# Re-laid seams between three phases of a spectral-mixer block, and its output bias added by VectorE

## The chip, the cores and the metric

The kernel runs on one core of a Trainium2 chip. The metric is the device time of one execution in microseconds (us), as the median of several runs. TensorE (PE) multiplies, VectorE (DVE) and ScalarE (ACT) work element by element, GpSimd (POOL) issues gathers and stores, and SyncE (SP) issues loads. Each engine takes its instructions strictly in order, and so does each DMA queue its issues.

## The reference, cut to what matters

The function is one transformer-like block, and the kernel computes its output and the gradients of all inputs. S is 2048 tokens, D 1024 channels, F 3584 hidden channels.

```python
h = _layernorm(x) * (1 + ca) + sa          # ca, sa, ga, cb, sb, gb: rows of silu(c) @ w_mod
x = x + ga * irfft2(rfft2(h) * W)          # W = w_r + 1j * w_i
h = _layernorm(x) * (1 + cb) + sb
y = _layernorm(h)
h = gelu(y @ w1 + b1)
x = x + gb * (h @ w2 + b2)                 # out_0; b2 is the output bias
```

Of the gradients, these matter here: that of row gb of the modulation is the sum over tokens of grad_out * (h @ w2 + b2); that of w2 is h^T @ (gb * grad_out); that of y is gz @ w1^T, where gz is the gradient ahead of the gelu.

## The kernel before, in words

The work goes through phases, all written as one program over four blocks b of 512 tokens (NB = 4, BW = 512); KH = 512 is half of the channels. The order of instructions on each engine is made by a scheduler from the order of the program, from priorities, and from explicit orderings: `ordered()` chains TensorE's products of the feed-forward phase (L650), `tc.high_priority()` lifts copies out of PSUM, `tc.issue_after` holds an instruction behind another. Tiles share memory by their tag, so a load into a new tile waits for the last reader of the old tile of that tag. PSUM has eight banks in three groups: `ps_s` (2), `ps_d` (2) and `ps_f` (4).

**Feed-forward, forward and local backward (L747 to L881).** `plan` (L853) is a list of steps. A "z" step (`z_block`, L762) computes one group of 512 hidden channels for a block: 32 products `pz` into four banks, copies by ScalarE (L779), then a long chain of ScalarE and VectorE for gelu and its derivative (L781 to L797), with stores of the hidden tile (`hh`, to d_hh) and of gz (to d_gz). A "b" step advances `bo_pass(b, h)` (L803), which multiplies hidden tiles by w2 for half h of the output channels. One pass has four banks `pbs`. It first adds the bias with four one-row products, one for each bank (L808: a row of ones times `b2_row`, a tile of one partition), then does seven groups of 16 products (L817), each with a w2 tile of 512 KB loaded into one of four slots `w2p` (L812). At the end ScalarE copies the banks to `bo` in the tile `otile` (L826), VectorE computes `go = grad_out * bo` (L827) and the output `bo * gb + x1` (L828, L829), which is stored. The second half of the generator, run later, sums `go` over tokens with four products `pa` against ones (L836), and VectorE adds the sum to `gacc` (L839, L841). These late parts are kept in `bo_late` and run at the first or second step of the next pass (L873); those of the last pass run at L879 and are followed by `store_gmod`, which sends gacc to memory as row 5 of d_gmod. `otile` is one tile, used by every pass.

**Gradient of y, the `pg` phase (L944 to L1029).** w1 is loaded transposed (L949). For each block and half, seven groups of 16 products `pg` (L996) accumulate in four `ps_f` banks from the gz tiles `gzr` (loaded at L989, eight slots) and w1T. ScalarE copies them out with sums (L1001), then VectorE runs two LayerNorm backwards (`ln_bwd`, L893, with L895 to L900 and L1017), and TensorE adds column sums of gn3, pru and au into the banks `acc3` (L193), placed by the scheduler among the next block's products. `got` is a scratch tile that also holds grad_out for the block (loads L128 on SP and two gathers L131 on POOL); `au` holds another operand. Beside this runs the "early" ring, `gmod_ring((5,), ...)` (L918): it loads row 5 of d_gmod to all partitions (L926), and goes through eight pieces of w_mod (L923), each with one VectorE product with a sum (L934), one scaled copy (L936) and a store by POOL (L937).

**Gradient of w2, the `gw2acc` phase (L1032 on).** Four tiles `gB` hold gb * grad_out, one for each block: loads on SP (L128), gathers on POOL (L131), then one VectorE product (L1037). They use the memory of w1T_0 to w1T_3, so each load waits until `pg` has last read that part. The generator `pieces()` (L1113) gives the work in pieces that `fill(n)` places between other phases: for each of 28 slices `fc` of the hidden channels, a transposing load of a 512 KB slice of d_hh (`hh_load`, L1115, on SP), and for each half h 16 products over the 16 token tiles t (L1090), tiles 4b to 4b+3 from gB block b, followed by a copy and a store. At the end of `pg` come six such pieces, then the last column sums (`sums3`), then ten pieces, then the backward spectral phase, which begins with the products `pu` (L451).

Of the kernel before, what the change touches and what calls it, by code (L numbers as in the profile page):

```python
# [11 lines left out]
BF16 = mybir.dt.bfloat16  # L12
I32 = mybir.dt.int32
ACT = mybir.ActivationFunctionType
ALU = mybir.AluOpType
AX = mybir.AxisListType

P = 128
S = 2048
D = 1024  # L20
# [10 lines left out]
NB = 4  # L31
# [4 lines left out]
def kernel(  # L36
# [135 lines left out]
    def tt(out, a, b, op):  # L172
        return nc.vector.tensor_tensor(out=out, in0=a, in1=b, op=op)  # L173
# [476 lines left out]
    def ordered():  # L650
        return tc.issue_after(last_pe[0].ins)
# [92 lines left out]
    n3Ts = [reg.tile([P, NDC, BW], BF16, name="n3Ta", tag="uv3")]  # L744
    otile = []

    b2_row = small.tile([1, D], BF16, name="b2_row", tag="gmrow", bufs=1)  # L747

    def after_ph():
        nc.sync.dma_start(out=b2_row[:], in_=B_b2.rearrange("(o n) -> o n", o=1))  # L750
        t2, t3 = (reg.tile([P, 2, 4, BW], BF16, name=f"gt{k}", tag=f"t{k}") for k in (2, 3))
        gts.append([t2[:, 0], t2[:, 1], t3[:, 0], t3[:, 1], uvp2[:, 0]])
        w2p.append(reg.tile([P, 4, BW], BF16, name="w2sB", tag="ph")[:])
        n3Ts.append(reg.tile([P, NDC, BW], BF16, name="n3Tb", tag="wt"))
        otile.append(reg.tile([P, 3, 4, BW], BF16, name="otile", tag="ot"))
# [47 lines left out]
    def bo_pass(b, h):  # L803
        cs_ = slice(h * KH, (h + 1) * KH)
        pbs = [(ps_f if b < NB - 1 or h == 0 else (ps_s, ps_d)[k % 2])("pbo") for k in range(4)]
        for i in range(4):
            with ordered():
                last_pe[0] = nc.tensor.matmul(pbs[i][:], lhsT=ones_bf[0:1, :], rhs=b2_row[0:1, cs_], start=True, stop=False)  # L808
        for g in range(7):
            wp = w2p[w2n[0] % 4]  # L810
            w2n[0] += 1
            nc.sync.dma_start(out=wp, in_=w2_v[:, g * 4:(g + 1) * 4, cs_])  # L812
            hh = hh_slots[(b * 7 + g) % 11]
            for i in range(4):
                for k in range(4):
                    with ordered():
                        last_pe[0] = nc.tensor.matmul(pbs[i][:], lhsT=hh[:, k, i * P:(i + 1) * P], rhs=wp[:, k, :],  # L817
                                                      start=False, stop=(g == 6 and k == 3))
            if g < 6:
                yield  # L820
        bo, x1t, go = (otile[0][:, k] for k in range(3))
        nc.sync.dma_start(out=x1t, in_=chunk_rows(d_x1, b)[:, :, cs_])
        load_tok_half(go, grad_out, b, h)
        for i in range(4):
            with tc.high_priority():
                last_ev[0] = nc.scalar.copy(out=bo[:, i, :], in_=pbs[i][:])  # L826
        tt(go, go, bo, ALU.mult)  # L827
        tt(bo, bo, bcn(gb_row[:, cs_], 4), ALU.mult)  # L828
        tt(bo, bo, x1t, ALU.add)  # L829
        store_tok_half(out_0, bo, b, h)  # L830

        yield
        pa = (ps_d if b < NB - 1 else ps_f)("pa")
        for i in range(4):
            with ordered():
                last_pe[0] = nc.tensor.matmul(pa[:], lhsT=ones_bf[:], rhs=go[:, i, :], start=(i == 0), stop=(i == 3))  # L836
        with tc.high_priority():
            if b == 0:
                nc.vector.tensor_copy(out=gacc[:, cs_], in_=pa[0:1, :])  # L839
            else:  # L840
                tt(gacc[:, cs_], gacc[:, cs_], pa[0:1, :], ALU.add)  # L841
# [19 lines left out]
    for kind, b, g in plan:  # L861
        if kind == "z":
            z_block(b, g, g + 1)
        elif kind == "p":
            with ordered():
                ph_part(b, (2, 3))
            if b == NFC - 1:
                after_ph()
        else:
            if g == 0:  # L870
                boq[b] = bo_both(b)
            next(boq[b])
            if bo_late and g % 7 in (1, 2):  # L873
                for late in bo_late:
                    next(late, None)
                bo_late.clear()
            if g == 13:
                next(boq[b], None)
    for late in bo_late:  # L879
        next(late, None)  # L880
    store_gmod([gacc[:, 0:KH], gacc[:, KH:D]], 5)  # L881

    gb1 = small.tile([P, NFC], FP32, tag="gb1", bufs=1)
    nc.vector.reduce_sum(out=gb1[:], in_=gb1_acc[:], axis=AX.X)
    gb1_bf = small.tile([P, NFC], BF16, tag="b1_bf", bufs=1)
# [67 lines left out]
    n3u = reg.tile([P, 4, D], BF16, name="n3u", tag="uv1")  # L953
    n2u = reg.tile([P, 4, D], BF16, name="n2u", tag="uv2")
    pru = reg.tile([P, 4, D], BF16, name="pru", tag="uv3")[:]
    got = reg.tile([P, 6, D], BF16, name="got", tag="ot")
    fbuf2 = reg.tile([P, 4, 4, D], BF16, name="fbuf2", tag="fr")
    acc3 = [ps_d("acc3a"), ps_d("acc3b")]
    gzn = 0
    gmw = reg.tile([P, 2, D], BF16, name="gmw", tag="ph")  # L960
    gmg = reg.tile([P, 2, D], BF16, name="gmg", tag="sb")
    early = gmod_ring((5,), [gmw[:, 0], gmw[:, 1], gmg[:, 0]], gmg[:, 1, :])
    next(early)
    au = reg.tile([P, 4, D], BF16, name="au", tag="px1")

    fold2_in = {}

# [9 lines left out]
    for b in range(NB):  # L977
        gn3 = gn3s[b % 2]
        sums = small.tile([P, 2, 4], FP32, tag="sums")
        gzt = []  # L980
        nc.sync.dma_start(out=n3u[:], in_=chunk_rows(d_n3, b))
        nc.sync.dma_start(out=n2u[:], in_=chunk_rows(d_x1, b))
        norm_act(n2u, n2u, 1, b)
        go4 = got[:, 0:4, :]
        load_tok(go4, grad_out, b)
        for g in range(7):
            sl = gzr[gzn % 8 // 2][:, gzn % 2]
            gzn += 1
            nc.sync.dma_start(out=sl, in_=d_gz_v[:, g * 4:(g + 1) * 4, b * BW:(b + 1) * BW])  # L989
            gzt.append(sl)  # L990
        for h in range(2):
            pgs = [ps_f("pg") for _ in range(4)]
            for g in range(7):
                for i in range(4):
                    for k in range(4):
                        nc.tensor.matmul(pgs[i][:], lhsT=gzt[g][:, k, i * P:(i + 1) * P],  # L996
                                         rhs=w1Ts[g][:, k, h * KH:(h + 1) * KH],
                                         start=(g == 0 and k == 0), stop=(g == 6 and k == 3))
            for i in range(4):
                with tc.high_priority():  # L1000
                    nc.scalar.activation(out=gn3[:, i, h * KH:(h + 1) * KH], in_=pgs[i][:], func=ACT.Identity,  # L1001
                                         accum_out=sums[:, h, i:i + 1])
        tt(sums[:, 0, :], sums[:, 0, :], sums[:, 1, :], ALU.add)
        for i in range(4):
            t = 4 * b + i
            ln_bwd(gn3[:, i, :], sums[:, 0, i:i + 1], n3u[:, i, :], stats[:, 2, 0, t:t + 1], gn3[:, i, :], got[:, 4 + i % 2, :])
        next(early, None)
        tt(pru, gn3[:], n2u[:], ALU.mult)
        g2, ftmp = gn3, pru
        if b < NB - 1:  # L1010
            sums3(b, gn3, pru)
        else:
            g2, ftmp = gn3s[0], gzr[0].rearrange("p a b (c d) -> p (a b c d)", c=1).rearrange("p (q d) -> p q d", d=D)
        s2c = small.tile([P, 4], FP32, tag="s2c")
        for i in range(4):
            t = 4 * b + i
            nc.vector.tensor_tensor_reduce(out=g2[:, i, :], in0=gn3[:, i, :], in1=opcb_row, scale=1.0, scalar=0.0,  # L1017
                                           op0=ALU.mult, op1=ALU.add, accum_out=s2c[:, i:i + 1])
            ln_bwd(g2[:, i, :], s2c[:, i:i + 1], n2u[:, i, :], stats[:, 1, 0, t:t + 1], g2[:, i, :], got[:, 4 + i % 2, :])
        next(early, None)  # L1020
        tt(g2[:], g2[:], go4, ALU.add)
        nc.gpsimd.dma_start(out=chunk_rows(d_gx1, b), in_=g2[:])
        nc.sync.dma_start(out=au[:], in_=chunk_rows(d_A, b))
        tt(n3u[:], g2[:], bcn(ga_row, 4), ALU.mult)
        fold_tok(n3u, ftmp)
        fold2_in[b] = fold_d(fbuf2[:, b], n3u[:], ftmp)
        tt(au[:], g2[:], au[:], ALU.mult)
        if b < NB - 1:
            sums3_ga(b, au)  # L1029
            next(early, None)  # L1030
# [82 lines left out]
    def pieces():  # L1113
        def hh_load(fc):
            hh_in[0] = nc.sync.dma_start_transpose(out=hh_s[hh_o[fc]], in_=d_hh[fc * P:(fc + 1) * P, :])  # L1115

        hh_load(0)
        yield
        hh_load(1)
        for fc in range(NFC):  # L1120
            if fc + 2 < NFC:
                hh_load(fc + 2)
            for h in range(2 if fc < NFC - 2 else 0):
                acc = ps_f("gw2acc")
                for t in range(NT):
                    gw2_mm(acc, fc, h, t)
                gw2_out(acc, fc, h)
                yield
# [43 lines left out]

    next(todo)
    with tc.issue_after(gb_in.ins):
        fill(6)
    for cl in (CE, SE, CO, SO):
        nc.sync.dma_start(out=(smA2, smB2)[cl % 2][:, cl // 2], in_=d_SF[:, cl])
    sums3(3, gn3s[1], pru)
    fill(10)
    nc.sync.dma_start(out=em2, in_=d_E[:, 0])  # L1180

    def mid_bwd():
# [74 lines left out]
```

## Time and profile before

| quantity | value |
|---|---|
| median of 5 runs | 1523.6 us (1522.12 to 1525.98) |
| profiled execution, its own time | 1521.72 us |
| its span, first to last instruction | 1519.6 us |
| mean granted TensorE clock | 0.984 |
| busy: PE, DVE, ACT, POOL | 1430.1, 1072.8, 721.9, 362.3 us |
| feed-forward phase | about 346 to 771 us |
| pg phase | 776.6 to 993.8 us |
| gw2acc pieces before the spectral phase | 993.8 to 1064 us |

The profile shows one execution. A row of the time line has a start, a length, the engine, the line of the code, the operation with output and input tile, and a count of merged instructions; in brackets stand idle time of the engine ahead of it and what ended it. Matmuls overlap, so the length of a merged row runs a little into the next; the distance between starts is what counts. About one matmul record in fifty is missing, which lowers a count without any time lost. SPq and POOLq rows are issues of DMAs, whose data lands some microseconds later.

### The profile page before, as it was taken

To read this page: it belongs to the slowest core of one execution; us is meant where nothing else is said; L and a number is where in the kernel's file an instruction comes from. 1 tells how busy PE (TensorE), PEld (TensorE's weight loads), DVE (VectorE), ACT (ScalarE), POOL (GpSimd) and SP (SyncE) were. 2 spreads that over 40 slices of the span, in tenths; PEclk is the share of its full clock that TensorE was granted. 3 is DMA by queue.
4 is the path that set the end of the run, shared out by engine and by line. 5 is a ranking of instruction groups with operands and counts; after the bars stand their busy time and mean duration, and the time that the engine had idled before them with its cause. 6 is when DMAs were issued, how large, how long until landed. Compare 5 with 4: busy or idle time off the path is not lost.

```text
span 1519.6 us, 18221 instructions
## 1 busy us (share of the span) xinstructions
PE 1430.1 (94%) x6697; PEld 667.3 (44%) x6831; DVE 1072.8 (71%) x1577; ACT 721.9 (48%) x956; POOL 362.3 (24%) x428
## 2 busy tenths in 40 slices
PE   5889899999999999999989999979998999999998
PEld 2434445444444444444434444434444444444443
DVE  5992869897799887877224977876166666897642
ACT  4765556668886666656012333332522434443211
POOL 5720621111112122221210101311033421322422
PEclk8999999999999999999999999989999999999999
DMA  9972755989587876999955426595298976866993
GB/s 328 285 203 70 178 163 176 276 262 344 191 262 235 223 241 227 242 292 273 335 183 184 154 82 221 130 272 160 63 201 225 251 231 173 202 173 166 269 273 116
DMA packets 358160, 324.27 MB, mean 213 GB/s; under 512 B 209187, under 2 KB 300849, under 8 KB 357816
## 3 DMA queue, kind: packets, MB, share of 16 engines
q1 hardware_dynamic: 324184, 207.71, 51.6%
q0 software_dynamic: 33888, 115.41, 22.2%
q8 instruction: 53, 0.87, 0.2%
q14 instruction: 35, 0.29, 0.1%
HBM read 164.15 MB, written 109.10 MB: 180 GB/s over the span
## 4 chain that ended last, share of the span: by engine, by line
PE 47%; DVE 23%; issue 10%; DMA 8%; ACT 7%; POOL 3%; SPq 1%; POOLq 0%; DVEq 0%; ACTq 0%
PE gw2acc L1090 10%; PE pbo L817 9%; PE pz L776 7%; PE pg L996 5%; DVE ct L173 4%; PE pv L544 3%; PE pp L659 3%; PE pu L451 3%; DVE gt L173 2%; PE gw1acc L1157 2%; DVE got L895 2%; DVE gn3a L900 1%; DMA out_dram<-otl 1%; DMA gB<-in_grad_out_dram 1%; DMA xt<-d_gx 1%
## 5 line engine op out<-in xcount | busy, mean ns | idle before, releaser
L659 PE MATMUL pp<-gBoT,wt 128*128 128x512 bf16 x874 | 198.1, 379 | 3.0 <-DMA wt<-in_B_w_dram 0.9
L996 PE MATMUL pg<-w1T,gzr 128*128 128x512 bf16 x884 | 196.0, 381 | 1.1
L1157 PE MATMUL gw1acc<-gzh,n3n 128*128 128x512 bf16 x875 | 195.1, 379 | 1.1
L776 PEld LDWEIGHTS <-w 128*128 128x128 bf16 x896 | 87.6, 98 | 109.4 <-issue 4.1
L996 PEld LDWEIGHTS <-gzr 128*128 128x128 bf16 x896 | 88.0, 98 | 107.8 <-issue 3.1
L1157 PEld LDWEIGHTS <-n3n 128*128 128x128 bf16 x896 | 87.6, 98 | 103.7
L659 PEld LDWEIGHTS <-wt 128*128 128x128 bf16 x896 | 87.4, 98 | 103.5 <-issue 1.7
L776 PE MATMUL pz<-n3Tb,w 128*128 128x512 bf16 x439 | 98.7, 379 | 1.9 <-DVE w2sD L839 1.5
L776 PE MATMUL pz<-n3Ta,w 128*128 128x512 bf16 x440 | 98.4, 379 | 2.2 <-ACT gt L779 1.3
L1090 PE MATMUL gw2acc<-gB,hhsA 128*128 128x512 bf16 x438 | 98.9, 379 | 0.5
L817 PEld LDWEIGHTS <-hhA 128*128 128x128 bf16 x608 | 59.5, 98 | 76.1 <-issue 6.9
L1095 ACT CAST gwo<-gw2acc 128x512 bf16<-128x512 f32 x54 | 30.6, 584 | 127.4 <-PE gw2acc L1090 85.5
L779 ACT ACTIVATE gt<-pz,b_col 128x512 bf16<-128x512 f32 x112 | 72.8, 683 | 28.9 <-PE pz L776 25.3
L785 ACT ACTIVATE gt<-gt 128x2048 bf16<-128x2048 bf16 x28 | 53.4, 1910 | 65.6 <-DVE gt L173 65.4
L173 DVE TENSOR_TENSOR gt<-gt,gt 128x2048 bf16<-128x2048 bf16 x56 | 68.4, 1223 | 15.9 <-ACT gt L787 15.1
L1161 ACT CAST gwo<-gw1acc 128x512 bf16<-128x512 f32 x48 | 27.8, 583 | 108.1 <-PE gw1acc L1157 100.0
L173 DVE TENSOR_TENSOR ct<-ct 128x2048 bf16<-128x2048 bf16 x64 | 76.0, 1219 | 0.8
L1090 PE MATMUL gw2acc<-gB,hht 128*128 128x512 bf16 x250 | 59.2, 395 | 8.0 <-DVE gB L173 7.5
L1090 PEld LDWEIGHTS <-hhsA 128*128 128x128 bf16 x448 | 43.8, 98 | 50.4
L781 ACT ACTIVATE gt<-gt 128x2048 bf16<-128x2048 bf16 x28 | 53.5, 1910 | 7.6 <-DVE gb_acc L796 6.9
L787 ACT ACTIVATE gt<-gt 128x2048 bf16<-128x2048 bf16 x28 | 53.3, 1908 | 0.4
L1162 POOL DMA_DIRECT2D out_dram<-gwo x56 | 30.5, 546 | 80.7 <-ACT gwo L1161 52.0
(314 smaller groups left out, 2546.5 us busy)
## 6 DMA issues: line engine op xcount, KB each, us to landing
gzr<-d_gz SPq DMA_DIRECT2D x28, 512.0 KB, 8.0
wblk<-in_w_mod_dram SPq DMA_DIRECT2D x12, 1024.0 KB, 13.4
d_ph<-pho POOLq DMA_DIRECT2D x21, 512.0 KB, 5.1
out_dram<-otl POOLq DMA_DIRECT2D x40, 256.0 KB, 3.6
d_hh<-hhA POOLq DMA_DIRECT2D x19, 512.0 KB, 4.8
w2sD<-in_B_w_dram SPq DMA_DIRECT2D x14, 512.0 KB, 6.3
hhC<-d_ph SPq DMA_DIRECT2D x14, 512.0 KB, 5.8
w2sA<-d_ph SPq DMA_DIRECT2D x14, 512.0 KB, 3.8
```

The costliest lines, as they stand in the source:

```text
L173: return nc.vector.tensor_tensor(out=out, in0=a, in1=b, op=op)
L451: last_pu[0] = nc.tensor.matmul(pu[:], lhsT=fb[:, i, cl, c8 * P:(c8 + 1) * P], rhs=sm[:, i, :], start=(i == 0), stop=(i == 3))
L659: last_pe[0] = nc.tensor.matmul(pp[:], lhsT=wt[:, fg % 2, cch, k * P:(k + 1) * P], rhs=gBoT[j][:, cch, :], start=(cch == 0), stop=(cch == ...
L776: last_pe[0] = nc.tensor.matmul(pz[:], lhsT=w1s[g][:, cch, k * P:(k + 1) * P], rhs=n3T[:, cch, :], start=(cch == 0), stop=(cch == NDC - 1))
L779: nc.scalar.activation(out=zb[:, k, :], in_=pz[:], func=ACT.Identity, bias=b1_col[:, fc:fc + 1], scale=1.0)
L781: nc.scalar.activation(out=av, in_=zb, func=ACT.Square)
L785: nc.scalar.activation(out=sg, in_=bv, func=ACT.Sigmoid, scale=2.0 * GK)
L787: nc.scalar.activation(out=bv, in_=bv, func=ACT.Sigmoid, scale=-2.0 * GK)
L817: last_pe[0] = nc.tensor.matmul(pbs[i][:], lhsT=hh[:, k, i * P:(i + 1) * P], rhs=wp[:, k, :], start=False, stop=(g == 6 and k == 3))
L996: nc.tensor.matmul(pgs[i][:], lhsT=gzt[g][:, k, i * P:(i + 1) * P], rhs=w1Ts[g][:, k, h * KH:(h + 1) * KH], start=(g == 0 and k == 0), sto ...
L1090: nc.tensor.matmul(acc[:], lhsT=hh_s[hh_o[fc]][:, t, :], rhs=gBs[t // 4][:, t % 4, h * KH:(h + 1) * KH], start=(t == 0), stop=(t == NT - 1))
L1157: nc.tensor.matmul(acc[:], lhsT=n3ns[t // 4][:, t % 4, cch * P:(cch + 1) * P], rhs=gz2[t // 8][:, t % 8, :], start=(t == 0), stop=(t == NT ...
```

## The change: what it does

1. `b2_row` becomes a tile of 128 partitions, loaded by a broadcast. The 32 one-row products (L808) go; the first product of each bank starts the accumulation. VectorE adds the row to the copied tile `bo`, once in a pass, ahead of L827.
2. The late part of a pass (`pa`) runs at step 3 of the next pass in place of steps 1 or 2. That of the last pass, and `store_gmod` for row 5, move from the end of the feed-forward phase into the pg phase, behind the 112 products of its first half. It takes a `ps_s` bank. The first step of the early ring, the tiles `got` and `au` and the first load of `got` move there with it.
3. The first two slices of the gw2acc phase are interleaved: four accumulators (two slices, two halves, two `ps_s` and two `ps_f` banks) go through gB block 0, then block 1, and so on. Both slices of d_hh are loaded before the first product. `fill(6)` and `fill(10)` become `fill(8)` and `fill(8)`, so 32 products more stand ahead of the last column sums.

In the scheduled program the first two transposing loads of the gw2acc phase stand on SP behind the first and the second gB load, with au, n3u and the last two gB loads after them; before, the second stood behind all four gB loads. The w_mod loads of the early ring stand between the gzr loads of block 1; before, they stood ahead of them. In the last passes some w2 loads change places with gzr loads. The sums of pru in block 0 come 9 `pg` products later, those of au 2 more, and the following ones return to their place.

```diff
-    b2_row = small.tile([1, D], BF16, name="b2_row", tag="gmrow", bufs=1)
+    b2_row = small.tile([P, D], BF16, name="b2_row", tag="gmrow", bufs=1)
...
-        nc.sync.dma_start(out=b2_row[:], in_=B_b2.rearrange("(o n) -> o n", o=1))
+        nc.sync.dma_start(out=b2_row[:], in_=B_b2.partition_broadcast(P))
...
-        for i in range(4):
-            with ordered():
-                last_pe[0] = nc.tensor.matmul(pbs[i][:], lhsT=ones_bf[0:1, :], rhs=b2_row[0:1, cs_], start=True, stop=False)
...
-                                                      start=False, stop=(g == 6 and k == 3))
+                                                      start=(g == 0 and k == 0), stop=(g == 6 and k == 3))
...
+        tt(bo, bo, bcn(b2_row[:, cs_], 4), ALU.add)
         tt(go, go, bo, ALU.mult)
...
-        pa = (ps_d if b < NB - 1 else ps_f)("pa")
+        pa = (ps_s if b == NB - 1 and h == 1 else ps_d if b < NB - 1 else ps_f)("pa")
...
-            if bo_late and g % 7 in (1, 2):
+            if bo_late and g % 7 == 3:
...
-    for late in bo_late:
-        next(late, None)
-    store_gmod([gacc[:, 0:KH], gacc[:, KH:D]], 5)
...
-    got = reg.tile([P, 6, D], BF16, name="got", tag="ot")
...
-    next(early)
-    au = reg.tile([P, 4, D], BF16, name="au", tag="px1")
...
-        go4 = got[:, 0:4, :]
-        load_tok(go4, grad_out, b)
+        if b > 0:
+            load_tok(got[:, 0:4, :], grad_out, b)
...
+            if b == 0 and h == 0:
+                for late in bo_late:
+                    next(late, None)
+                store_gmod([gacc[:, 0:KH], gacc[:, KH:D]], 5)
+                next(early)
+                got = reg.tile([P, 6, D], BF16, name="got", tag="ot")
+                au = reg.tile([P, 4, D], BF16, name="au", tag="px1")
+                load_tok(got[:, 0:4, :], grad_out, b)
...
         hh_load(0)
-        yield
         hh_load(1)
+        yield
         for fc in range(NFC):
             if fc + 2 < NFC:
                 hh_load(fc + 2)
-            for h in range(2 if fc < NFC - 2 else 0):
+            if fc == 1:
+                first = [(f_, h, (ps_s, ps_f)[f_]("gw2acc")) for f_ in range(2) for h in range(2)]
+                for b in range(NB):
+                    for f_, h, acc in first:
+                        for t in range(4 * b, 4 * b + 4):
+                            gw2_mm(acc, f_, h, t)
+                    if b < NB - 1:
+                        yield
+                for f_, h, acc in first:
+                    gw2_out(acc, f_, h)
+                yield
+            for h in range(2 if 1 < fc < NFC - 2 else 0):
...
-        fill(6)
+        fill(8)
...
-    fill(10)
+    fill(8)
```

## The prediction, on record before the result

> **What bounds the kernel now.** I read the page's busy times first, then what TensorE waited for in the two stages that the change touches, then the seams on the time line, TensorE alone.
>
> ```profile
> PE 1430.1 (94%) x6697; PEld 667.3 (44%) x6831; DVE 1072.8 (71%) x1577; ACT 721.9 (48%) x956; POOL 362.3 (24%) x428
> ```
>
> TensorE is busy 94% of the span, and the chain that ended last runs mostly through it (47%). So the change is worth what it does to TensorE's instructions and to its idle time. The waits of TensorE between 380 and 1015 us (total, times, longest), without those that the time line shows below and a small one that stays:
>
> ```profile
> PE gw2acc L1090 <- DVE gB L173: 7.5, 3, 5.0
> PE pa L836 <- DVE otile L173: 3.6, 1, 3.6
> ...
> PE pz L776 <- DVE w2sD L839: 1.8, 2, 1.5
> ...
> PE pz L776 <- ACT gt L779: 1.3, 1, 1.3
> ```
>
> The first three stand where the change edits, the fourth behind the first group that it removes. The time line shows what each costs (start, duration, work, idle before it):
>
> ```profile
> 713.18 0.60 PE L808 MATMUL pbo<-b_row,ones_bf 1*128 1x512 bf16 x2
> 715.63 0.86 PE L808 MATMUL pbo<-b_row,ones_bf 1*128 1x512 bf16 x2 [1.85 <-ACT otile L826]
> 716.42 5.31 PE L817 MATMUL pbo<-w2sD,hhA 128*128 128x512 bf16 x16
> 721.57 3.62 PE L817 MATMUL pbo<-w2sB,hhB 128*128 128x512 bf16 x15
> ...
> 743.45 1.03 PE L808 MATMUL pbo<-b_row,ones_bf 1*128 1x512 bf16 x4
> 745.94 3.61 PE L817 MATMUL pbo<-w2sC,hhA 128*128 128x512 bf16 x15 [1.46 <-DMA w2sC<-in_B_w_dram]
> ```
>
> ```profile
> 771.33 0.23 PE L188 MATMUL ptr<-fin,gb_bf 128*28 128x128 bf16 x1 [0.18 <-ACT otile L826]
> 775.17 1.62 PE L836 MATMUL pa<-otile,ones_bf 128*128 128x512 bf16 x4 [3.62 <-DVE otile L173]
> 776.58 23.75 PE L996 MATMUL pg<-w1T,gzr 128*128 128x512 bf16 x102
> ```
>
> ```profile
> 993.83 1.03 PE L1090 MATMUL gw2acc<-gB,hht 128*128 128x512 bf16 x4
> 995.18 1.02 PE L1090 MATMUL gw2acc<-gB,hht 128*128 128x512 bf16 x4 [0.32 <-DVE gB L173]
> 1001.23 1.87 PE L1090 MATMUL gw2acc<-gB,hht 128*128 128x512 bf16 x4 [5.04 <-DVE gB L173]
> 1005.27 3.57 PE L1090 MATMUL gw2acc<-gB,hht 128*128 128x512 bf16 x8 [2.17 <-DVE gB L173]
> ```
>
> A full product takes 0.216 us (16 from 721.57 fill 3.45). After an idle stretch it takes 0.43: the four from 1001.23 took 1.87.
>
> **The change part by part,** in before's coordinates.
>
> *Bias products (L808).* Four per pass, eight passes. The group at 743.45 takes 4 x 0.216 = 0.86 us though it has one row; others 0.96 to the next work. The pass (0,0) gains nothing: the pz at 414.72 waits for ScalarE, which waits for VectorE, so TensorE only arrives earlier at that wait. Passes (1,0) to (2,1) lie where TensorE has no gap but single missing records: 4 x 0.9 = 3.6 us. Pass (0,1) goes with the next item, (3,0) and (3,1) with the one after.
>
> *Bias add on VectorE.* Eight more 128x2048 adds with a broadcast row. The existing twin (otile<-otile,rows) takes 1.22 us, so 9.8 us of VectorE. Pa, its only reader on TensorE, moves one or two steps of 3.45 us later, which covers 1.22. Uncovered is the dense stretch around 455: from 440 to 460 VectorE is busy 19.93 of 20 us. Bounds 0 to 2.4 (two adds); I take 0.4. The 256 KB load of the row, in place of 2 KB, is issued at 108.6, and the SP queue is idle until 135.7: nothing.
>
> *Pa one step later.* The 1.5 us wait at 471.80, for a bank that VectorE had yet to read after pa, goes, because VectorE's backlog ends at 481.5 and pa then comes near 488. With (0,1)'s 0.9 that is 2.4; ScalarE's copies of the following z blocks have only 0 to 3 us in hand, so 2.0 after the 0.4. Bounds 0.5 to 2.4.
>
> *Passes (3,0) and (3,1).* From 713.18 to 721.57 run 16 needed products, 3.45 us, so 4.9 are lost: 0.86 of bias, about 2 of wait for two banks (copied at 715.0, behind a sigmoid), 2 of half rate. Now the third bank is first touched eight products in, at 714.9, and waits 0.7 to 1.0 until 715.6; the gain is 3.9 (bounds 1.2 to 4.3). At 743.45 the bias hides 0.86 of a wait for w2sC. In the new order of the SP queue that load stands ahead of two 512 KB gzr loads that it stood behind, but TensorE comes 4 us earlier, and the DMA share from 720 to 740 is 1.06: of 2.3 (0.86 and 1.46) I take 1.2 (bounds 0.5 to 2.3). Sum 5.1.
>
> *First seam.* Pg follows ptr at 771.5 instead of 776.58; the four pa (0.86) come after 112 pg. That is 4.2 us. What is late next: (a) ScalarE's copies of the last pass, which ptr needs, stand behind an activation that waits for the n2u load (landed 769.5). That load now stands behind a load that waits for pa: about 1.3 us later. (b) The early ring (L934, L936) starts 24.2 us later, since pa feeds it. From pa to its first round were 10.9 us, now 1.2 less; rounds were 14.5 and 8.9 apart, the longer one held by gathers on POOL that now come sooner. So the third round, two products of 1.15, comes at about 823.2, between the LayerNorm products of block 0, which reach that place at 822.6. Together 3.4 us late; the new TensorE order puts the sums that depend on it 9 and then 2 pg (2.4) later; 1.0 remains. The ring's w_mod loads also stand between the gzr loads of block 1 on SP, but the last is due 20 us after it goes out. The got load and its two gathers, held until pa (796), are first needed at 820, au at 856. Net 4.2 - 1.3 - 1.0 = 1.9. Bounds -4 to 4.2.
>
> *Second seam.* Four accumulators now share each gB block: 16 products, 3.45 us, in place of 4. From 993.83 some 20 products were done by 1009.06, 10.8 us more than their need. If gB2 and gB3 are ready as before (1001.2, 1005.2), 64 products end at 1008.7 against 1018.5: 9.8 gained. But hh piece 1 must be there at once, and its transpose now stands ahead of gB2 and gB3 on SP:
>
> ```profile
> 971.65 6.86 SPq L1115 DMA_TRANSPOSE hht<-d_hh  x1
> 978.60 0.53 SPq L128 DMA_DIRECT2D gB<-in_grad_out_dram  x1
> 979.23 1.10 SPq L1023 DMA_DIRECT2D au<-d_A  x1
> 980.42 1.43 SPq L128 DMA_DIRECT2D gB<-in_grad_out_dram  x1
> 982.30 0.44 SPq L981 DMA_DIRECT2D n3u<-d_n  x1
> 983.66 7.57 SPq L128 DMA_DIRECT2D gB<-in_grad_out_dram  x1
> ```
>
> In 5 us windows from 970 to 1005 the DMA share is 0.92 to 1.31, so another 512 KB transpose costs all behind it some 3.5 us (an unhindered one's issue, at 1126) to 6.9. gB3 landed at 1002.8, now near 1007; gB2, now behind au and n3u, just ahead of it, near 1005.6 instead of 998.9. Then block 2 starts at 1008, at half rate (6.9 us), block 3 follows, and 64 products end near 1019: -0.5. I take 0, nearest to the queue rows; bounds -4 to 9.8. VectorE's chain of block 3 then runs 5 us later, under the 13 us between its end (1051) and pu (1064); its first sums move 32 products (6.9) later.
>
> The Trainium skill, DMA: Bandwidth & Descriptors, Latency and other measured facts, gives DMA transposes 261 GB/s. By that 512 KB would be an estimated 2.0 us, and the second seam would gain about 3 more; the 6.86 us row speaks against it here.
>
> The Trainium skill, TensorE: Matmul & The Clock Gate, What's actually happening, has the clock back after one busy window of about 3.4 us. Here products ran at 0.43 us until 1009, 7.8 us after 1001.23; by the page's rule the restart would cost some 1.7 us less in the second seam.
>
> **Sum.** 3.6 + 2.0 + 5.1 + 1.9 + 0 = 12.6 us. The profiled execution took 1521.72 (span 1519.6 and 2.1 around it), so 1509.1; the median of the runs shown, 1523.6, is 1.9 above it: **1511**. All best: 3.6 + 2.4 + 6.6 + 4.2 + 9.8 = 26.6; all worst: 3.6 + 0.5 + 1.7 - 4 - 4 = -2.2.
>
> **Rivals.**
> 1. *The second seam pays in full.* For it: bulk loads on POOL's queue are not behind the transpose. Against it: au and n3u ahead of gB2. 1511 - 9.8 = 1501. Chance 0.13.
> 2. *The waits only move.* VectorE and ScalarE in the dense stretch, the full DMA engines before 745 and the n2u load take what the removed products give; only the four middle passes and 1 to 2 us remain, and the second seam costs 3 or 4. That the change doesn't do what it says is this case: 1519 to 1525. For it: a DMA share of 1.09 and 1.06 from 700 to 740; against it: fewer loads ahead of w2sC. Chance 0.17, of which 0.06 still below 1520.5.
> 3. *The early ring holds block 0: slower.* Its third round stands inside VectorE's in-order stream; each us past 822.6 beyond 2.4 delays the sums and then TensorE, one for one. It decides the sign when the round comes 13 us later than I have it (after 836), as it would if its rounds took over 15 us each; at 20 us each it comes at 845 and costs 22 more: 1533. For it: the 14.5 us round; against it: 8.9 with POOL free. Chance 0.08.
>
> **How the numbers follow.** The forecast (1503 to 1518) has 0.62. Faster by over 0.2%, about 3 us and the least that a measurement of this kernel can tell from none, is 0.62 + 0.13 + 0.06 = 0.81; within 0.2% 0.11; slower 0.08. The range 1501 to 1520 takes in rival 1 and the near edge of rival 2.
>
> **What would show it.** No L808; TensorE's groups follow within 1 us at 713 and 743; no wait at 471; pg directly behind ptr; pa amid pg without a wait. Right about the second seam: gB2 and gB3 land together, one wait of 5 to 8 us, then 0.43 us products. Wrong: that wait under 1 us (1501), or an acc3 wait of over 5 us in block 0 (slower).

## The result and the profile after

The changed kernel takes 1534.0 us (median of 42 runs), the kernel before 1524.7 (79 runs): 1.0062 of before, 95% interval 1.0051 to 1.0073. It is slower by some 9.4 us; 1511 was forecast. The profiled execution took 1532.5 with a span of 1530.2, 10.6 more than before's.

The busy times on the page:

```profile
PE 1422.9 (93%) x6666; PEld 665.3 (43%) x6799; DVE 1080.3 (71%) x1585; ACT 719.8 (47%) x956; POOL 363.2 (24%) x428
```

TensorE works 7.2 us less and VectorE 7.5 more, as planned, yet the span grew: the loss is idle TensorE. What TensorE waited for between 380 and 1015 us (total, times, longest):

```profile
PE acc3a L193 <- DVE gn3a L894: 8.5, 1, 8.5
PE pbo L814 <- DMA w2sA<-in_B_w_dram: 4.9, 1, 4.9
PE gw2acc L1089 <- DVE gB L173: 3.9, 1, 3.9
PE pz L776 <- DVE w2sD L837: 3.6, 2, 2.2
PE pz L776 <- ACT gt L779: 2.7, 3, 1.4
...
PE gw2acc L1089 <- DMA hht<-d_hh: 2.1, 1, 2.1
PE ptr L188 <- ACT otile L823: 2.0, 1, 2.0
```

The first, second, sixth and seventh were not there before, or under 0.3. The fourth was 1.8 and the fifth 1.3. The third fell from 7.5. One by one:

*First group of block 3's first pass* (TensorE's time line: start, duration, work, idle before it):

```profile
710.53 1.89 PE L814 MATMUL pbo<-w2sD,hhA 128*128 128x512 bf16 x7
713.08 1.89 PE L814 MATMUL pbo<-w2sD,hhA 128*128 128x512 bf16 x8 [0.66 <-ACT otile L823]
714.80 3.62 PE L814 MATMUL pbo<-w2sB,hhB 128*128 128x512 bf16 x16
723.32 4.87 PE L814 MATMUL pbo<-w2sA,hhB 128*128 128x512 bf16 x14 [4.90 <-DMA w2sA<-in_B_w_dram]
```

and the queue of SP (issues, us until the next can go):

```profile
707.85 8.61 SPq L943 DMA_TRANSPOSE w1T<-in_B_w_dram  x4
716.57 0.52 SPq L980 DMA_DIRECT2D gzr<-d_gz  x1
717.18 0.60 SPq L809 DMA_DIRECT2D w2sA<-in_B_w_dram  x1
```

and the same load in before:

```profile
716.37 0.45 SPq L812 DMA_DIRECT2D w2sA<-in_B_w_dram  x1
```

TensorE leaves the groups with w2sD and w2sB 6.8 us earlier than before, and then waits 4.9 for w2sA, whose load goes out at 717.18, behind four w1T transposes as in before. There it went out at 716.37, landed 5.4 us later and was first needed at 725.89: it landed under the removed products and waits.

*Block 0 in the pg stage.* TensorE, then VectorE (the ring is L928 and L930, the LayerNorm L889 to L894; a round is one of the ring's eight pieces of w_mod here and in the experiments, while the prediction calls a group of up to three pieces a round):

```profile
820.81 6.85 PE L987 MATMUL pg<-w1T,gzr 128*128 128x512 bf16 x31
836.17 0.58 PE L193 MATMUL acc3a<-gn3a,sel 128*128 128x512 bf16 x1 [8.51 <-DVE gn3a L894]
...
836.98 10.21 PE L987 MATMUL pg<-w1T,gzr 128*128 128x512 bf16 x39
```

```profile
808.51 1.23 DVE L928 CUSTOM_DVE_ANT_0 gmw<-gmw,gmg 128x1024 bf16<-128x1024 bf16 x1 [9.47 <-DMA gmg<-d_gmod]
...
818.20 1.23 DVE L928 CUSTOM_DVE_ANT_0 gmw<-gmw,gmg 128x1024 bf16<-128x1024 bf16 x1 [4.86 <-DMA gmw<-in_w_mod_dram]
...
823.65 1.23 DVE L928 CUSTOM_DVE_ANT_0 gmg<-gmg 128x1024 bf16<-128x1024 bf16 x1 [1.41 <-DMA gmg<-in_w_mod_dram]
...
825.32 1.22 DVE L889 CUSTOM_DVE_ANT_0 got<-gn3a,n3u 128x1024 bf16<-128x1024 bf16 x1
...
829.33 1.22 DVE L928 CUSTOM_DVE_ANT_0 gmw<-gmw,gmg 128x1024 bf16<-128x1024 bf16 x1 [1.40 <-DMA gmw<-in_w_mod_dram]
...
832.11 1.22 DVE L928 CUSTOM_DVE_ANT_0 gmw<-gmw,gmg 128x1024 bf16<-128x1024 bf16 x1 [1.47 <-DMA gmw<-in_w_mod_dram]
...
834.84 2.48 DVE L894 SCALAR_TENSOR_TENSOR gn3a<-gn3a,stats,got 128x1024 bf16<-128x1024 bf16 x2 [0.33 <-ACT got L893]
```

In VectorE's order all eight rounds stand ahead of the first write of gn3a. From 818.20 on each of them waits for its w_mod load, and LayerNorm behind them waits too: gn3a is written at 834.84, against 828.75 in before, though pg began 5.6 earlier. In before the ring was done at 812.6, ahead of the LayerNorm.

*Second seam:*

```profile
1000.00 1.89 PE L1089 MATMUL gw2acc<-gB,hht 128*128 128x512 bf16 x7
1003.96 5.35 PE L1089 MATMUL gw2acc<-gB,hht 128*128 128x512 bf16 x24 [2.06 <-DMA hht<-d_hh]
1013.17 7.03 PE L1089 MATMUL gw2acc<-gB,hht 128*128 128x512 bf16 x23 [3.86 <-DVE gB L173]
```

```profile
977.83 7.12 SPq L1114 DMA_TRANSPOSE hht<-d_hh  x1
985.03 0.53 SPq L128 DMA_DIRECT2D gB<-in_grad_out_dram  x1
985.62 12.03 SPq L1114 DMA_TRANSPOSE hht<-d_hh  x1
...
1000.61 2.55 SPq L128 DMA_DIRECT2D gB<-in_grad_out_dram  x2
```

The second transpose holds the queue for 12.03 us, and the loads of gB2 and gB3 stand behind it. Even so the seam itself gains: from the first gw2acc product to the first pu are 66.65 us, against 70.36 in before.

*The first pu.* That gain is lost again there. POOL's gathers (L470) wait for `fbuf`, which VectorE writes at the end of block 3's chain. In before:

```profile
1051.36 1.01 POOL L470 DMA_INDIRECT ws<-in_A_w_r_dram,xu  x1 [6.22 <-DVE fbuf L173]
```

and after, with what follows on POOL, ScalarE and TensorE:

```profile
1062.74 1.01 POOL L470 DMA_INDIRECT ws<-in_A_w_r_dram,xu  x1 [12.67 <-DVE fbuf L173]
...
1067.55 1.15 POOL L1096 DMA_DIRECT2D out_dram<-gwo  x2
```

```profile
1070.13 1.07 ACT L1094 CAST gwo<-gw2acc 128x512 bf16<-128x512 f32 x2 [9.54 <-DMA out_dram<-gwo]
```

```profile
1071.74 8.54 PE L451 MATMUL pu<-smA,fbuf 128*128 128x512 bf16 x30 [3.20 <-ACT U L622]
```

The gathers go out 11.4 us later, 5.2 more than the 6.2 by which the pg stage ends later. The stores of gwo stand behind them on POOL, ScalarE's copies of gwo wait for these stores, and pu's copies (L622) stand behind those. So pu waits 3.2, and with the slow products after it the first half of pu takes 5.1 more.

### The profile page after: what moved, and what is told of

The parts are those of the page before. It is cut to its first block, busy times and chain, and to the rows that moved or that the text cites. A ratio compares the mean times of both kernels' runs of the same rounds, so it can differ in the third digit from the quotient of the medians.

```text
span 1530.2 us, 18161 instructions
## 1 busy us (share of the span) xinstructions
PE 1422.9 (93%) x6666; PEld 665.3 (43%) x6799; DVE 1080.3 (71%) x1585; ACT 719.8 (47%) x956; POOL 363.2 (24%) x428
## 4 chain that ended last, share of the span: by engine, by line
issue 13%; PE 13%; DVE 10%; DMA 9%; POOL 3%; ACT 2%; SPq 1%; POOLq 0%; ACTq 0%; DVEq 0%
PE gw2acc L1089 4%; PE pg L987 2%; PE gw1acc L1167 2%; PE pu L451 2%; DVE ct L173 1%; DMA xt<-d_gx 1%; DVE got L889 1%; DMA out_dram<-pf 1%; DMA out_dram<-otl 1%; DVE gn3b L894 1%; PE pv L544 1%; DMA out_dram<-gwo 1%; DMA gB<-in_grad_out_dram,xu 1%; DMA gB<-in_grad_out_dram 1%; DVE ct L1072 1%
## 5 line engine op out<-in xcount | busy, mean ns | idle before, releaser
L659 PEld LDWEIGHTS <-wt 128*128 128x128 bf16 x896 | 87.3, 98 | 103.3 <-issue 1.5
L776 PE MATMUL pz<-n3Tb,w 128*128 128x512 bf16 x439 | 98.5, 379 | 2.1 <-DVE w2sD L837 1.4
L928 DVE CUSTOM_DVE_ANT_0 otl<-otl 128x1024 bf16<-128x1024 bf16 x16 | 19.1, 1222 | 45.1 <-DMA otl<-in_w_mod_dram 37.2
```

What stands on the lines that cost most here:

```text
L659: last_pe[0] = nc.tensor.matmul(pp[:], lhsT=wt[:, fg % 2, cch, k * P:(k + 1) * P], rhs=gBoT[j][:, cch, :], start=(cch == 0), stop=(cch == ...
L776: last_pe[0] = nc.tensor.matmul(pz[:], lhsT=w1s[g][:, cch, k * P:(k + 1) * P], rhs=n3T[:, cch, :], start=(cch == 0), stop=(cch == NDC - 1))
```

## The experiments

Each kernel ran in five rounds beside before. The table adds what one trace of each shows, in us between marks that TensorE's groups give: *z* from the first pbo to the last pz, *last* to the first pg, *pg* to the last pg, *seam 2* to the last pu of the first s_fwd half (1093.5 in before), *rest* to the last product, in stages that the edits hardly touch.

| kernel | z | last | pg | seam 2 | rest | ratio to before, 95% |
|---|---|---|---|---|---|---|
| before | 318.2 | 70.4 | 217.2 | 99.7 | 419.8 | 1 |
| changed | 315.5 | 67.4 | 229.0 | 101.0 | 422.6 | 1.0062 (1.0051–1.0073) |
| no_bias_part | 318.4 | 65.1 | 223.9 | 98.5 | 419.0 | 1.0028 (1.0005–1.0052) |
| no_seam1 | 315.5 | 73.7 | 218.3 | 99.0 | 424.4 | 1.0045 (1.0022–1.0068) |
| no_seam2 | 315.8 | 65.8 | 226.3 | 99.3 | 421.6 | 1.0041 (1.0019–1.0063) |
| ring_late | 315.6 | 65.5 | 227.2 | 104.2 | 422.6 | 1.0085 (1.0052–1.0117) |
| ring_held | 317.5 | 67.6 | 228.9 | 103.3 | 422.6 | 1.0082 (1.0056–1.0107) |
| ring_tail | 317.0 | 67.5 | 229.6 | 94.6 | 423.0 | 1.0017 (0.9994–1.0039) |
| ring_end | 317.6 | 68.0 | 218.5 | 103.2 | 420.8 | 1.0048 (1.0023–1.0073) |
| bias_only | 315.0 | 75.4 | 217.9 | 100.5 | 415.9 | 1.0048 (1.0024–1.0072) |
| products_gone | 316.6 | 70.0 | 216.9 | 102.7 | 425.7 | 1.0011 (0.9992–1.0030) |
| add_only | 322.5 | 72.3 | 217.6 | 98.2 | 417.5 | 1.0053 (1.0030–1.0077) |
| add_twice | 318.3 | 84.9 | 216.8 | 100.6 | 428.3 | 1.0095 (1.0058–1.0133) |
| bias_mid | 315.5 | 73.2 | 216.8 | 100.4 | 422.0 | 1.0002 (0.9980–1.0024) |
| add_block3 | 317.7 | 74.2 | 217.0 | 100.3 | 421.2 | 1.0013 (0.9994–1.0032) |
| load_only | 317.6 | 71.7 | 216.1 | 99.7 | 425.3 | 1.0009 (0.9988–1.0031) |
| seam1_ring_tail | 318.1 | 66.2 | 227.5 | 96.1 | 420.7 | 0.9999 (0.9980–1.0018) |
| seam1_ring_end | 318.0 | 67.6 | 217.0 | 99.8 | 424.4 | 1.0006 (0.9983–1.0029) |
| mid_seam1_ring_end | 315.1 | 70.4 | 217.0 | 99.1 | 421.5 | 1.0012 (0.9988–1.0037) |
| s12_ring_end | 317.7 | 64.5 | 217.0 | 107.1 | 426.1 | 1.0036 (1.0012–1.0060) |

How to read it: executions of one kernel spread by 8 to 22 us, and the last stages alone by 12 from trace to trace. So a stage tells *where* something is lost in one execution, the ratio *whether* the time moved; 0.001 is 1.5 us. The difference of two ratios has an interval of some 0.0025 to 0.0035 (4 to 5 us) either way, an estimate from the intervals in the table.

### One part undone

no_seam1 has before's text of the first seam, no_seam2 before's hh_load order and `fill(6)`, `fill(10)`, no_bias_part the one-row products and no add (each the reverse of its hunks in the diff above).

no_seam1: 

> The changed kernel with the first seam as before (last pa, its row's store, the early ring's loads and the got and au tiles ahead of pg); bias, pa step 3 and second seam stay. Theory R: what the first seam gave (pg 3.6 us earlier of the 5.6 in the trace) goes, and the 8.5 us wait and the half-rate stretch after it (11.7 us in all by 250 to 300 products of pg) go too, so it is 5 to 8 us faster than the changed kernel: 1526 to 1529. Rival S2 (the loss sits in the second seam and what follows it): about 4 us slower than the changed kernel, 1537 to 1539.

no_seam2: 

> The changed kernel with the second seam as before (four accumulators one after another, hh piece 1 loaded after the first step, 6 and 10 groups). Theory R: the second seam itself gave 0 us in the trace (its offset is +6.2 at both ends), and the later 4 us (a wait for ScalarE's gwo copy at 1068, waits for cs01b at 1239) come from the 2 groups that stand ahead of block 3's sums: 0 to 5 us faster than the changed kernel, 1529 to 1534. Rival S2 (the loss sits there): 8 us or more faster, 1526 or less. If the second seam did pay inside the delay of the first: slower, 1535 to 1540.

no_bias_part: 

> The changed kernel with the bias part undone (one-row products back, no VectorE add); pa step 3 and both seams stay. Rival B (the bias part is what makes it slower): 1526 to 1529, 5 us or more faster than the changed kernel. Theory R: the products cost TensorE 2.5 us up to the last pz, so it is as slow as the changed kernel or 1 to 3 us slower, 1534 to 1537.

Measured against the changed kernel: 2.6 us faster (0.0017), 3.2 (0.0021), 5.2 (0.0034). Each with an interval of some 4 us either way: no one part is the whole loss, and only the bias part's 5.2 is clear of nothing. Undoing the first seam gives back 10.7 us of pg stage and loses 6.3 ahead of it. For no_bias_part rival B's forecast held. Its trace is 5.1 us shorter in the pg stage, where the wait for gn3a is 5.9 and not 8.5, and 2.9 longer in *z*; but this execution was one of its fastest, so where the typical 5.2 lies is not shown.

### The early ring

ring_late, the first two of block 0's rounds left out of the text:

```diff
-        next(early, None)
+        if b > 0:
+            next(early, None)
```

> The changed kernel, with the two rounds of the early ring that stand inside block 0's LayerNorm chains on VectorE left out there (the ring still takes its eight rounds, in blocks 0 end, 1, 2 and 3). Theory R (the ring's late rounds hold block 0): TensorE's wait of 8.5 us for gn3a (at 827 to 836) shrinks below 2 us and the half-rate products after it go, so 8 to 11 us of the changed kernel's 1534 are saved, less 0 to 3 for rounds pushed into blocks 1 to 3: 1523 to 1529. Rival G (block 0's chain is late through the got and n3u/n2u loads and the gathers that now go out behind pa, not through the ring): the wait stays above 5 us, and the time is 1531 to 1535.

The wait stayed (8.2 us), which looked like rival G. But the scheduler, not the text, sets VectorE's order: in the trace all eight rounds still stood ahead of the first write of gn3a (ring_held's expectation counts four). The run separates nothing. ring_held binds them:

```diff
...
-        next(early, None)
+        if b == 0:
+            held = ln_in
+        with tc.issue_after(held.ins):
+            next(early, None)
...
```

> The changed kernel with all eight rounds of the early ring ordered behind block 0's second LayerNorm chain on VectorE (the run ring_late left rounds out of the text of block 0 only, and the scheduler put four of them ahead of the chain all the same). Theory R (the ring's rounds hold block 0): TensorE's wait of 7 to 9 us for gn3a at 825 goes to under 2 us, pg ends 8 to 11 us sooner than in the changed kernel's trace (989 to 992 instead of 1000), and the time is 1523 to 1528. Rival G (the chain waits for got, n3u or n2u): the wait stays above 5 us, 1531 to 1536. Rival B (the bias part costs some 6 us of its own by the runs so far, the seams little): the wait goes, but the time stays at 1528 to 1532, the level of the bias part alone.

TensorE's largest waits in ring_held, and the VectorE line of block 1 that answers to it:

```profile
PE acc3a L193 <- DVE gn3b L894: 8.3, 1, 8.3
...
PE acc3a L193 <- DVE gn3a L894: 1.0, 2, 0.8
```

```profile
883.05 1.23 DVE L928 CUSTOM_DVE_ANT_0 gmw<-gmw,gmg 128x1024 bf16<-128x1024 bf16 x1 [7.01 <-DMA gmw<-in_w_mod_dram]
```

Block 0's wait is gone, as theory R has it, but the ring now holds block 1: the same price one block later, and no gain. ring_tail puts 3, 3 and 2 rounds behind the second LayerNorm chain of blocks 0, 1, 2:

```diff
...
+        with tc.issue_after(ln_in.ins):
+            for _ in range(3):
+                next(early, None)
...
```

> The whole change, with the early ring's eight rounds ordered behind the second LayerNorm chain of each block (3, 3, 2 in blocks 0, 1, 2), so that no LayerNorm product stands behind a ring round that waits for its load; in ring_held the rounds left block 0 and held block 1's sums 8.5 us instead. Theory R (the ring in VectorE's order is the whole loss of the pg stage): no wait for gn3a or gn3b above 2 us in any block, the pg stage (first to last pg) takes 217 to 219 us as in before, not 227 to 229, and the time falls by 8 to 11 from the changed kernel's 1534: 1523 to 1526, which is still no better than before, since the add eats the products. Rival (the loads and gathers behind pa are late by themselves): a wait of 4 us or more stays, 1529 to 1534.

The time fell by 6.9 us (0.0045), short of the 8 to 11 of theory R, and its trace refutes the way: the pg stage stayed at 229.6, with waits of 4.5 and 4.3 in blocks 1 and 2. LayerNorm of block 1 waits for the load of n3u until 884.2; that this load is late because VectorE's work on block 0 ends later by its rounds is argued. The second seam was shorter in its place (94.6), the only one of the traces with the new seam that has no wait at the first pu. ring_end takes the rounds out of the pg stage and does the row among the last products:

```diff
...
-    for r in (2, 1, 0):
+    for r in (5, 2, 1, 0):
         gmod_row(r, w1g["ins"])
-        fill(8)
+        fill(6)
```

> The whole change, with the early ring's eight rounds taken out of the pg stage and done among the last products, where the rows 2, 1 and 0 are done (VectorE is busy 23 to 34 of 50 us there). Theory R (the ring, wherever it stands in the pg stage, is what the first seam costs): no wait for gn3a or gn3b above 2 us, pg stage 217 to 219 us, time 1523 to 1527. Rival G (the LayerNorm chains are late by their own loads, or TensorE's sums now stand too early in its order): waits of 4 us and more stay, pg stage above 224, and the time is 1528 to 1533.

```profile
PE acc3a L193 <- DVE au L173: 2.9, 3, 1.0
PE ptr L188 <- ACT otile L823: 2.4, 1, 2.4
...
PE acc3a L193 <- DVE gn3a L894: 0.2, 1, 0.2
```

These are ring_end's waits from 770 to 995; left out is pru (1.5 in three waits), and no other is longer than 0.2 us. The long ones for gn3a and gn3b have gone, and the stage is 218.5. That the ring makes the pg stage some 10.5 us longer is shown. That the time pays for it is not: the ratio, 1.0048, does not tell ring_end from the changed kernel. Its own profiled span, 1523.8, was 5 us below the mean span of its runs, so what the typical execution loses is not seen.

The same with the first seam alone, before's products and second seam:

seam1_ring_tail: 

> The kernel before with the first seam alone (last pa amid pg, row store, ring, got and au behind it) and the ring at the block ends as in ring_tail; one-row products kept, no add, second seam as before. If the first seam is worth the 5.4 us between the last pz and the first pg that the run no_bias_part shows, and the ring was all that it cost: 1517 to 1520, faster than before by 0.2 to 0.4%. If the rest of the seam (n2u load behind the w_mod loads, got and gathers late) takes it back: 1522 to 1526.

seam1_ring_end: 

> The kernel before with the first seam alone and the ring among the last products; one-row products and second seam as before. Theory R: the first seam's 4 to 6 us stay gained: 1517 to 1521. Rival G: 1523 to 1527. A third way: pg ends 5 us earlier, but the second seam waits for hh and gB by the SP queue and gives it back there: 1522 to 1524, with the pg stage at 217.

0.9999 and 1.0006: the same as before, and as each other, though their pg stages are 227.5 and 217.0. seam1_ring_end keeps the stage short and pg's end 3.2 us early by its trace, and still gains nothing that the time shows; its third way (given back at the second seam, where 8.3 us of waits for gB stand in place of 7.5) accounts for 1 us. Its last stages, where the ring now stands, are 4.6 longer than before's, which is within their spread; so the place of this loss stays open.

### The bias part

bias_only is the hunk of the bias alone; products_gone drops the products without an add; add_only adds and keeps the products; load_only is the row's load to 128 partitions; add_twice:

```diff
-        tt(bo, bo, bcn(b2_row[:, cs_], 4), ALU.add)
+        for _ in range(2):
+            tt(bo, bo, bcn(b2_row[:, cs_], 4), ALU.add)
```

bias_mid and add_block3 make the add conditional on `b < NB - 1` (products in block 3 alone) and `b == NB - 1` (products everywhere).

bias_only: 

> The kernel before with the bias part alone: no one-row products, the row broadcast and added by VectorE; pa stays in step 1 or 2, both seams as before. The prediction's terms for it: 3.6 for the middle passes, 0.5 for pass (0,1), 3.9 and 0.9 for the last two passes, with 0.4 off for VectorE: about 8 less than before, 1516. Theory W (the waits only move: z stage paced by ScalarE and VectorE, w2 load behind the w1T transposes at 718): 1.5 to 3 us less than before, as the last pz (-2.5) and last pbo (-2.3) stood in the changed kernel's trace: 1521.5 to 1523.

products_gone: 

> The kernel before without the one-row products and without any add (the bias is left out). If the add is what costs: 1518 to 1523, the 2.5 to 8 us of removed products. If losing the products costs (idle at the w2 loads, lower clock): 1527 to 1532, as the bias part alone.

add_only: 

> The kernel before with the broadcast row and its add on VectorE put in, and the one-row products kept (the bias is added twice). Separates the two halves of the bias part, which alone measured 1.0048 of before. If the add costs (eight adds of 1.2 us on VectorE and the chain copy, add, multiply, pa at the seam): 1528 to 1532. If the cost is that TensorE lost its products and now idles at w2 loads and drops its clock: 1523 to 1527, the 1.2 us of the seam at most.

load_only: 

> The kernel before with the output bias loaded to all 128 partitions (256 KB in place of 2 KB), products kept, no add. Prediction: nothing, 1523 to 1525. If the load is what costs: 1528 or more.

add_twice: 

> The kernel before with the bias part, and each of the eight adds done twice (the bias counts twice). If the adds set the time (by bias_only 7 us for eight): 14 to 16 us above before, 1537 to 1540. If the add costs only the two at the seam, 1.2 us each and what the clock adds: 1 to 3 us above bias_only, 1529 to 1533. If the adds cost nothing and bias_only's 1.0048 was mostly spread from run to run: 1524 to 1527.

bias_mid: 

> The kernel before with VectorE's add in place of the products in blocks 0 to 2 and the products kept in block 3's two passes. If the add costs in the last passes and at the seam (where copy, add, multiply and pa stand in one chain and TensorE meets the w2 loads): the 2.7 us of the middle stay gained and the last passes are as before, 1520.5 to 1523. If it costs in the z stage, where VectorE is busy 19.9 of 20 us: 1526 to 1531, as the bias part alone.

add_block3: 

> The kernel before with VectorE's bias add in block 3's two passes alone, all products kept (the bias counts twice in block 3). If the add costs at the seam, in the chain copy, add, multiply, pa: 1527 to 1531 by the medians of add_only; the trace should then show pg 1.5 to 3 us later than before and the rest behind it. If it costs in the z stage: 1523 to 1525.5.

Both forecasts for bias_only missed: slower by 7. Dropping the 32 products gains nothing that shows (products_gone, at most 1.2 us); the add costs 8 (add_only), and adding twice 14 (9 to 20), twice bias_only's 7. The load costs nothing that shows. So VectorE's add is the price. The traces put it ahead of the first pg, which comes 2.3 us later than in before in bias_only, 6.3 in add_only and 15.0 in add_twice. Within that they differ: it is the last passes in bias_only and add_twice (75.4 and 84.9 in *last*, against 70.4), but mostly the z stage in add_only (322.5, against 318.2). TensorE's waits from 388 to 800 in bias_only and in add_twice, where before had 3.6 for pa:

```profile
PE pa L834 <- DVE otile L173: 6.1, 3, 4.9
PE pbo L814 <- DMA w2sA<-in_B_w_dram: 3.8, 1, 3.8
PE pbo L814 <- DMA w2sD<-in_B_w_dram: 2.8, 2, 1.7
...
PE ptr L188 <- ACT otile L823: 2.2, 1, 2.2
```

```profile
PE pa L835 <- DVE otile L173: 15.9, 3, 6.1
```

The add stands between ScalarE's copy and the product that pa reads, where pa follows one step later or at once. The parts do not add up, though: the add in blocks 0 to 2 costs nothing (1.0002), in block 3 alone 2 us (1.0013, not told from 0), in all eight passes 7 to 8. bias_only's trace explains 3.8 of 7 us (to the last pu); the remainder stays open. bias_mid's *last* is 73.2 with the products kept there. In the changed kernel pa comes later and waits 0.3 in all, for ScalarE; there the add's cost is not located.

### Joined versions

mid_seam1_ring_end joins bias_mid and seam1_ring_end; s12_ring_end has both seams, products, and the ring at the end.

mid_seam1_ring_end: 

> The kernel before with the add in place of the products in blocks 0 to 2, the first seam, and the ring among the last products; second seam as before. If each part keeps what its own run showed: theory R 1516 to 1520, faster than both kernels; if the last passes wait for their w2 loads whatever comes before: the same as seam1_ring_end within 1.5 us.

s12_ring_end: 

> The kernel before with both seams and the ring among the last products; products kept, no add, pa steps as before. If the second seam is worth nothing: as seam1_ring_end, 1522 to 1526. If it pays once the pg stage is not delayed: 1516 to 1520. If it costs the 2 to 4 us that the waits for gB and for gwo's copy ahead of pu show: 1526 to 1529.

mid_seam1_ring_end equals before (1.0012), so nothing tried beats before. In its trace the z stage is 2.9 shorter than in seam1_ring_end and *last* 2.8 longer: the products' gain is waited away at the w2 loads and at ptr. s12_ring_end is 4.6 us slower than seam1_ring_end, with an interval of some 5; its waits from 975 to 1100 show where its trace loses:

```profile
PE gw2acc L1084 <- DMA hht<-d_hh: 8.4, 1, 8.4
PE pu L451 <- ACT U L622: 3.2, 1, 3.2
PE gw2acc L1084 <- DVE gB L173: 2.3, 1, 2.3
```

Its pg ends earliest of all (986.4), and it waits longest for hh piece 1; in the other traces with this seam that wait is 0 to 4.3. The 3.2 at pu are those of the changed kernel: POOL's gathers wait 12.68 for block 3's chain here too, the gwo stores stand behind them, and a copy of gwo waits 9.56 for such a store. seam1_ring_end and no_seam2, with the second seam as before, have no wait at pu. A wait of 5.8 for gzh among the last products, where the ring now stands, is a further part of its loss (1.3 in seam1_ring_end, the same ring).

## Why the prediction was wrong, step by step

- *Bias products, middle passes, 3.6.* With the next term 5.6 were due in the z stage. The last pz comes 2.7 sooner in *z* (3.2 in bias_only, add counted), and 0.6 to 2.7 in the other versions of the changed kernel without the products: less than forecast, by how much one trace cannot say.
- *Pa one step later, 2.0.* Failed; 0 or less. The wait for the bank at 471.80 went, and two came:

```profile
492.39 0.81 PE L776 MATMUL pz<-n3Tb,w 128*128 128x512 bf16 x3 [1.42 <-DVE w2sD L837]
...
547.37 1.89 PE L776 MATMUL pz<-n3Ta,w 128*128 128x512 bf16 x8 [2.15 <-DVE w2sD L837]
```

  The step "VectorE's backlog ends at 481.5 and pa then comes near 488" took the backlog's end for lasting; at 491.66 pa's copy stood between gb_acc reductions of the next group.
- *Passes (3,0) and (3,1), 5.1.* Failed; 0. The third bank's wait was 0.66, as forecast, and the wait for w2sC in the second pass went. But the 3.9 counted TensorE's own work and not the next load: w2sA, under cover in before until 725.89, became a 4.9 us wait. The last pbo is 2.3 earlier, no more than the z stage had given. That is rival 2, for this stage.
- *First seam, 1.9.* The 4.2 less 1.3 for n2u is 2.9; pg came 5.6 earlier, of which the last pbo had 2.3, so 3.3: right, with ptr's wait of 2.0 in it. The failing step is (b), where the third round "comes at about 823.2" and "1.0 remains". In the prediction's sense of a round, its gaps of 8.9 put the three at 805.4, 814.3 and 823.2; they came at 808.5, 818 to 824, and 829 to 832. The first began 7.1 us after the load of row 5 went out (5.1 in before). For the others SP waits, as in before, until the ring's own stores have freed its three buffers:

```profile
811.59 1.17 POOL L931 DMA_DIRECT2D out_dram<-gmw  x2 [10.40 <-DVE gmw L930]
```

```profile
813.99 3.40 SPq L917 DMA_DIRECT2D gmw<-in_w_mod_dram  x2
```

  Each round then starts 3.2 to 5.7 us after its w_mod load went out, with 512 KB gzr loads among these loads; in before the second and third group started 2.7 and 3.5 us after theirs. And the second round stood ahead of the LayerNorm too, where only the third was counted. So rival 3's mechanism came although its point (third round after 836) was not reached. With it came the sign that the prediction had named for being slower, an acc3 wait of over 5 us in block 0: 8.5 us of wait, then TensorE slow. Its products start 0.43 us apart until 839.90, with a granted clock of 0.52 from 836 to 840, and 0.22 apart after that, at a clock of 1.00: 1.8 us lost from 836.17 on. The Trainium skill, TensorE: Matmul & The Clock Gate, What's actually happening, has the clock back after a busy window of some 3.4 us. At half rate that window loses an estimated 1.7, which this stretch of 3.7 us bears out, while the prediction had set a longer one (7.8 us, with pauses in it) against it.
- *Second seam, 0.* By the trace -1.3, of two parts: 3.7 gained up to the first pu, 5.1 lost from there to the end of its half. The failing step is "under the 13 us between its end (1051) and pu (1064)": it set VectorE's chain of block 3 against pu alone and put what waits for that chain on POOL at nothing, the gathers and the gwo stores behind them. By the runs the cost is 3.2 (no_seam2) and 4.6 (s12_ring_end against seam1_ring_end), near the lower bound of -4, but each interval reaches 0. The forecast "one wait of 5 to 8 us" came as two, 2.1 for hh piece 1 and 3.9 for gB. By the Trainium skill, DMA: Bandwidth & Descriptors, Latency and other measured facts (261 GB/s for DMA transposes with a non-contiguous middle dimension), piece 1 would be an estimated 2.0 us of transfer. Its issue held SP 12.03 us here, so the measurement decides.
- *VectorE's add, 0.4.* Mis-sized most of all: 8 us in add_only (4.6 to 11.7), where pa stands as in before. In the changed kernel its cover, that pa "moves one or two steps of 3.45 us later", held for pa, which waited 0.3; but the bias part still costs 5.2 there, where the prediction had it gain, so the cover of one wait was not the whole price.

Forecast 12.6 gained; the trace has 10.6 lost. To the first pg the kernel was ahead by 5.6 where 13.6 were due (all terms but the ring's 1.0); the pg stage took 11.8, the second seam with pu 1.3, the later stages 2.8, which is within their spread. By the runs without one part, the bias part costs 5.2, the second seam 3.2 and the first 2.6, the last two not told from nothing; where the bias part's cost lies in the changed kernel's typical execution stays open.

## What to carry to other kernels

Removing work from an engine gained nothing here where the issue time of the next load decided: before counting a gain, follow the queue of the following loads and ask what lands last. A background job on an in-order engine must have its inputs landed before its place, or it holds the foreground by the time of its loads; moved within that stage it left the stage as long (229 us), out of it the stage was 10.5 shorter, but the time showed no gain. An add put between a copy and its reader is not free because its engine has idle time: here eight adds, 9.8 us of VectorE, cost 7 to 8 us of the whole. And work made later on one engine delays what stands behind its readers in other queues: here stores on POOL, and through them TensorE.

## What the runs showed of the hardware

The time of one kernel goes with TensorE's mean granted clock: over 30 runs of before beside the first experiments, 0.001 less clock went with 1.2 us more; which of the two is the cause is not shown. After the wait of 2.06 us at the second seam the granted clock was 1.00 (1004 to 1009), after the one of 3.86 us it was 0.50 (1014 to 1017). A 512 KB transpose of d_hh held SP's queue for 6.86 us in before, 7.12 and 12.03 in the changed kernel, and 3.54 later in before (at 1126). And one trace is no median: in bias_only the profiled span was 1519.5, the mean span of its runs 1528.5.
